# Attention scores with tokens on the partitions in a fused attention and expert kernel

## The chip, the cores and the metric

The kernel runs on 1 core of one Trainium2 chip. The metric is the device time of one execution in microseconds (us): the median of several runs of the kernel before is 1126.33 us (three runs, 1125.7 to 1126.88). One more execution was recorded by the hardware profiler, and every row shown below comes from that one.

## The reference, cut to what matters

Three layers follow one another. The change touches only the first, an attention over 32 memory slots. The inputs q, k and phi are the drawn ones times 64, 64 and 2.859.

```python
# q, k, v: (4, 8, 576, 64)   phi: (4, 8, 576, 32)   batch, head, token, dim / slot
a = softmax of phi over the 32 slots
k_m = einsum('bhsm,bhsd->bhmd', a, k)
v_m = einsum('bhsm,bhsd->bhmd', a, v)
scores = scale * matmul(q, k_m^T)                 # (4, 8, 576, 32)
scores = scores - max(scores, axis=-1)
attn = exp(scores)
attn = attn / (sum(attn, axis=-1) + 1e-9)
x = matmul(attn, v_m)                             # then to (2304, 512)
# layer 2, 2304 tokens, 512 -> 2048 -> 512
h = maximum(x @ w_in, 0);  x = (h * h) @ w_out
# layer 3, four experts, 512 -> 1024 -> 512, weighted by the normalised domain_probs
out += p[:, e] * (maximum(x @ w1[e], 0) @ w2[e])
```

## The kernel before

The 32 pairs of batch and head are worked in eight groups g of four heads (two groups to a batch b). In each group 4 heads times 32 slots make 128 rows. The softmax of the scores runs over the 32 slots, so it wants the slots along the free dimension and the tokens on the partitions, while what the next layer reads (atts, the attention weights, split into a rounded part and a rest) wants the slots on the partitions and the 576 tokens along the free dimension.

A group is a generator in two parts. The first (letter F in the order below) is lines 131 to 184: the softmax of phi, its five transposes on TensorE (143), the memories k_m and v_m (150), their transposes (167), and the scores (180). The scores come out with the 128 rows of heads and slots on the partitions and 288 tokens at a time along the free dimension, in one bank of tag score and one of tag fold. VectorE turns each bank at once by 32x32 blocks into st (184), and both banks are free again. The second part (letter B) is lines 186 to 203: the maximum over 32 slots (187), its subtraction (188), the exponential on ScalarE (191), the sum (193), the division (194 to 196), the block transposes back into at (200), the rounded copy on ScalarE (202) and the rest of it (203). Lines 188 and 203 stand on GpSimd from group 4 on, line 196 from group 3 on.

PSUM has banks by tag: three of moe, one of turn, one of memory, one of score, two of fold.

The string PROGRAM orders stage 0. Its other letters are: W, one chunk of the weights of layer 2, turned from 64-bit floats by seven VectorE instructions (lines 217 to 229, some with a split at 244 and 245); A, fold(0, b), which multiplies v_m of a batch into w_in (344 to 351, two banks of tag fold); U, first(0, j), which runs layer 2 on 288 tokens for a slab of 256 hidden units: lines 372 to 381 (hidden units, their square and its split), and lines 393 to 399 (the product with w_out), put off in the list pend. A batch's U reads its folded weights and the atts of both of its groups. Stage 1 and later run layer 2 on the other slabs, in which no attention is left, and then layer 3.

The loads run in one queue, SyncE's: phi (99), k and v (115), q (124), 64-bit weights (237). The string FIRST_LOADS names the first ten, and the function front(g) issues those of a group that are not yet there.

The program text gives the order in which work is offered. The order on each engine is the framework's plan: in the trace VectorE has instructions of W, of B and of U mixed. On each engine instructions then run strictly in the planned order.

The shares p of the experts are loaded behind stage 0 (770) and normalised by four small VectorE instructions (773 to 776). They are read in layer 3 alone.

Of the kernel before, what the change touches and what calls it, by code (L numbers as in the profile page):

```python
# [31 lines left out]
NB = 512  # L32
# [7 lines left out]
def tile_kernel(  # L40
# [24 lines left out]
    def bank(tag):  # L65
        return (ps if tag in ("moe", "score") else ps_one).tile([128, 512], F32, tag=tag, name=tag, bufs=BANKS[tag])
# [15 lines left out]
    yacc = acc.rearrange("p (k n) -> p k n", k=KT)  # L82


    FIRST_LOADS = "p0 p1 r0 k0 r1 q1 q0 k1 r2 r3"

    PROGRAM = (
        "F0 W W F1 W W B0 A0 B1 F2 F3 U0 U1 A1 B2 B3 F4 W B4 F5 B5 A2 U2 U3 W "  # L90
        "F6 F7 U4 W B6 W A3 B7 U5 U6 U7"
    )


# [2 lines left out]
    def load_phi(att, g):  # L97
        ph = att.tile([128, S], F32, tag="ph", name=f"ph{g}", bufs=2)
        nc.sync.dma_start(out=ph, in_=phiT[g])
        return ph  # L100
# [27 lines left out]
    def attention(att, g):  # L128
# [43 lines left out]
            nc.scalar.copy(bt[rows, :, e * M:(e + 1) * M], ktv[rows, 0, :, e, :])  # L172
        rows = slice(hg * D, (hg + 1) * D)
        nc.scalar.copy(vt[rows, b], kt[rows, 128:])
        st = att.tile([128, S // 32, 32], F32, tag="st", name="st", bufs=2)
        stf = st.rearrange("p j m -> p (j m)")
        for z in range(2):
            sc = bank("score" if z == 0 else "fold")
            for pr in range(2):
                nc.tensor.matmul(  # L180
                    sc[pr * 64:(pr + 1) * 64, :HS], bt[:, pr, :], qt[pr][:, z * HS:(z + 1) * HS],
                    start=True, stop=True,
                )
            nc.vector.transpose(out=stf[:, z * HS:(z + 1) * HS], in_=sc[:, :HS])
        yield
        mx = att.tile([128, S // 32], F32, tag="mx", name="mx")
        nc.vector.reduce_max(out=mx, in_=st, axis=AX.X)
        (nc.gpsimd if g >= 4 else nc.vector).tensor_tensor(
            out=st, in0=st, in1=mx.unsqueeze(2).to_broadcast([128, S // 32, 32]), op=ALU.subtract
        )  # L190
        nc.scalar.activation(st, st, AF.Exp, scale=1.0 / math.sqrt(D))
        sm = att.tile([128, S // 32], F32, tag="sm", name="sm")
        nc.vector.reduce_sum(out=sm, in_=st, axis=AX.X)
        nc.vector.tensor_scalar_add(sm, sm, 1e-9)
        nc.vector.reciprocal(sm, sm)
        (nc.gpsimd if g >= 3 else nc.vector).tensor_tensor(
            out=st, in0=st, in1=sm.unsqueeze(2).to_broadcast([128, S // 32, 32]), op=ALU.mult
        )
        at = att.tile([128, S], F32, tag="at", name="at", bufs=1)
        nc.vector.transpose(out=at, in_=stf)  # L200
        hi = atts[b][:, hg]
        nc.scalar.copy(hi, at)
        (nc.gpsimd if g >= 4 else nc.vector).tensor_tensor(out=atts[b][:, 2 + hg], in0=at, in1=hi.bitcast(F32), op=ALU.subtract)  # L203

    F_MIN = float(np.array(896 << 20, np.uint32).view(np.float32))
    F_MAX = float(np.array((1150 << 20) | 0xFFFFF, np.uint32).view(np.float32))
# [517 lines left out]
    with tc.tile_pool(name="bdp", bufs=1) as bdp, tc.tile_pool(name="cv", bufs=1) as cv, \  # L727
# [5 lines left out]
            nc.gpsimd.memset(t, 0.0)  # L733
        with tc.tile_pool(name="att", bufs=2) as att, tc.tile_pool(name="hp1", bufs=2) as hp, \
                tc.tile_pool(name="tmp1", bufs=1) as tmp:
            at = {}

            def front(g):
                if g not in phs:
                    phs[g] = load_phi(att, g)  # L740
                if g not in kvs:
                    kvs[g] = load_kv(att, g)
                if g not in qs:
                    qs[g] = load_q(g)
                at[g] = attention(att, g)
                next(at[g])

            for t in FIRST_LOADS.split():
                i = int(t[1])
                if t[0] == "p":  # L750
                    phs[i] = load_phi(att, i)
                elif t[0] == "k":
                    kvs[i] = load_kv(att, i)
                elif t[0] == "q":
                    qs[i] = load_q(i)
                else:
                    raws[i] = load64(i)
            for t in PROGRAM.split():
                i = int(t[1]) if len(t) > 1 else 0
                if t[0] == "F":  # L760
                    front(i)
                elif t[0] == "B":
                    next(at[i], None)
                elif t[0] == "W":
                    next(ws)
                elif t[0] == "A":
                    fold(0, i)
                else:
                    first(0, i, (hp, tmp), lambda: bank("moe"))
            nc.sync.dma_start(out=p_sb, in_=probs)  # L770
            flush()

        nc.vector.reduce_sum(out=p_sum, in_=p_sb, axis=AX.X)
        nc.vector.tensor_scalar_add(p_sum, p_sum, 1e-9)
        nc.vector.reciprocal(p_sum, p_sum)
        nc.vector.tensor_tensor(
            out=p_sb, in0=p_sb, in1=p_sum.unsqueeze(2).to_broadcast([128, NT // 128, E]), op=ALU.mult
        )
        with tc.tile_pool(name="hp2", bufs=2) as hp, tc.tile_pool(name="tmp2", bufs=2) as tmp:
            bk = lambda: bank(next(CYCLE1))  # L780
            for b in range(B):
# [9 lines left out]
        with tc.tile_pool(name="ring", bufs=1) as rp, tc.tile_pool(name="tmp3", bufs=2) as tmp:  # L791
            ring = [rp.tile([128, KT, RING], F32R, name=f"ring{i}") for i in range(2)]
            for s in range(2, N1):
                last = s + 1 == N1
                for j in range(2 * B):
                    first(s, j, (ring, tmp), bk)
                    if not last:
# [130 lines left out]
```

## Time and profile before

| | before |
|---|---|
| median of three runs | 1126.33 us (1125.7 to 1126.88) |
| the profiled execution | 1126.93 us, span 1125.2 us |
| TensorE busy | 1098.6 us (98%) |
| VectorE busy | 854.3 us (76%) |
| ScalarE busy | 586.8 us (52%) |
| GpSimd busy | 21.0 us (2%) |
[...]

The span is what lies between the first and the last instruction; 1.7 us of the profiled execution lie outside it. A busy share says how much of a stretch an engine had an instruction in work. For TensorE the ends of matmuls are modelled, so a busy TensorE need not be one at full rate; the weight loads (PEld) are listed beside it. The rows in the section below come from views of this one trace: busy time by stretch, instructions in order of time, and groups of equal instructions.

### The profile page before, as it was taken

The numbers are of one execution on the slowest core, as the hardware profiler recorded it, in microseconds if no ns is written. First come the engines' busy times: TensorE is split into PE (matmuls) and PEld (weight loads), VectorE is DVE, ScalarE is ACT, GpSimd is POOL, SyncE is SP. The second block draws the span as 40 slices with busy tenths as digits, with TensorE's granted clock in tenths as the row PEclk, the third lists the DMA queues.
The fourth block names the chain that finished last, engine by engine and source line by source line (L and its number), as shares of the span: only waits on it lengthen the run. The fifth ranks groups of instructions, "written<-read, shape, count | busy, mean of one in ns | idle before, by whom it ended". The sixth has DMA issues, their size and how long they took to land.

```text
span 1125.2 us, 16430 instructions
## 1 busy us (share of the span) xinstructions
PE 1098.6 (98%) x6150; PEld 936.3 (83%) x6150; DVE 854.3 (76%) x1478; ACT 586.8 (52%) x1164; POOL 21.0 (2%) x22
## 2 busy tenths in 40 slices
PE   5899999999999999999999999999999999999998
PEld 3567898998999988888888888888888888888887
DVE  6898989886345768888898786866766677776767
ACT  3777665665456465444444443455554554554551
POOL 0032000000000000000000000000000000000000
PEclk9799999999999999999999999999999999999999
DMA  9761212221020068776777766455544555554423
GB/s 328 226 206 57 76 58 75 78 92 39 1 95 1 38 269 306 281 286 257 267 290 281 268 238 233 157 198 188 191 162 154 183 174 178 178 198 170 150 94 112
DMA packets 59727, 192.22 MB, mean 171 GB/s; under 512 B 6648, under 2 KB 8696, under 8 KB 59648
## 3 DMA queue, kind: packets, MB, share of 16 engines
q1 hardware_dynamic: 59648, 191.18, 47.9%
q8 instruction: 48, 0.79, 0.3%
q14 instruction: 31, 0.25, 0.1%
HBM read 119.31 MB, written 71.84 MB: 170 GB/s over the span
## 4 chain that ended last, share of the span: by engine, by line
PE 87%; DVE 7%; ACT 3%; DMA 1%; issue 1%; POOL 1%; SPq 0%; ACTq 0%; POOLq 0%
PE moe L519 23%; PE two L636 13%; PE fold L485 8%; PE moe L393 7%; PE two L671 4%; PE score L519 4%; PE two L690 4%; PE turn L485 4%; PE memory L485 4%; PE moe L372 3%; PE turn L393 3%; PE memory L393 2%; PE score L393 2%; PE memory L372 1%; PE fold L344 1%; PE score L372 1%
## 5 line engine op out<-in xcount | busy, mean ns | idle before, releaser
L519 PE MATMUL moe<-mem,f 128*128 128x512 f32 x576 | 146.1, 389 | 0.0
L519 PEld LDWEIGHTS moe<-mem,f 128*128 128x128 f32 x576 | 107.9, 188 | 22.6 <-DVE mem L412 0.2
L643 DVE TENSOR_TENSOR acc<-two,acc 128x1024 f32<-128x1024 f32 x56 | 68.6, 1224 | 64.3 <-PE two L636 63.7
L519 PE MATMUL moe<-mem,ws 128*128 128x512 f32 x384 | 98.0, 390 | 0.0
L485 PE MATMUL fold<-w,g 128*128 128x512 f32 x384 | 97.6, 389 | 0.0
L636 PE MATMUL two<-gt,f 128*128 128x512 f32 x360 | 88.9, 389 | 0.0
L485 PEld LDWEIGHTS fold<-w,g 128*128 128x128 f32 x384 | 72.1, 188 | 15.0
L519 PEld LDWEIGHTS moe<-mem,ws 128*128 128x128 f32 x384 | 71.8, 188 | 15.3 <-DVE c L565 0.2
L393 PE MATMUL moe<-ring,wo 128*128 128x384 f32 x432 | 80.9, 335 | 0.0
L636 PEld LDWEIGHTS two<-gt,f 128*128 128x128 f32 x360 | 67.6, 188 | 14.2
L641 ACT COPY acc<-two 128x1024 f32<-128x1024 f32 x49 | 49.6, 1013 | 50.4 <-PE two L636 50.4
L393 PEld LDWEIGHTS moe<-ring,wo 128*128 128x128 f32 x432 | 75.1, 188 | 0.0
L372 PE MATMUL moe<-mem 128*128 128x288 f32 x432 | 72.8, 303 | 1.4 <-POOL mem L203 0.8
L372 PEld LDWEIGHTS moe<-mem 128*128 128x128 f32 x432 | 62.1, 191 | 12.4 <-issue 6.5
L381 DVE TENSOR_TENSOR ring<-g,ring 128x288 fp32r<-128x288 f32 x96 | 43.3, 455 | 31.6 <-ACT ring L380 31.6
L379 ACT ACTIVATE g<-r 128x288 f32<-128x288 f32 x128 | 57.1, 446 | 4.0 <-DVE gl L381 2.2
L530 ACT COPY cc<-moe 128x512 f32<-128x512 f32 x65 | 38.3, 589 | 25.5 <-PE moe L519 25.5
L498 DVE SCALAR_TENSOR_TENSOR acc<-fold,p_sb,acc 128x512 f32<-128x512 f32 x60 | 44.8, 747 | 8.5 <-PE fold L485 8.2
L671 PEld LDWEIGHTS two<-mem,f 128*128 128x128 f32 x384 | 48.2, 191 | 1.2
L485 PE MATMUL turn<-w,g 128*128 128x512 f32 x192 | 49.0, 390 | 0.0
L519 PE MATMUL moe<-mem,w 128*128 128x512 f32 x192 | 48.9, 389 | 0.0
L485 PE MATMUL memory<-w,g 128*128 128x512 f32 x192 | 48.7, 389 | 0.0
(190 smaller groups left out, 2278.6 us busy)
## 6 DMA issues: line engine op xcount, KB each, us to landing
f<-kept SPq DMA_DIRECT2D x128, 512.0 KB, 4.0
kept<-w SPq DMA_DIRECT2D x64, 512.0 KB, 2.9
kept<-ws SPq DMA_DIRECT2D x32, 512.0 KB, 3.8
kept<-mem SPq DMA_DIRECT2D x32, 512.0 KB, 3.3
raw<-in_wts SPq DMA_DIRECT2D x28, 512.0 KB, 3.2
ra<-in_wts SPq DMA_DIRECT2D x16, 512.0 KB, 4.9
rb<-in_wts SPq DMA_DIRECT2D x16, 512.0 KB, 3.9
kv<-in_kv SPq DMA_DIRECT2D x24, 256.0 KB, 4.1
```

Of the source, the lines that this page charges most:

```text
L372: nc.tensor.matmul(ph[:, :HS], folded[b][:, lw + hg, fc], atts[b][:, rx + hg, cs], start=(i == 0), stop=(i == 5))
L379: nc.scalar.activation(g, r, AF.Square)
L381: nc.vector.tensor_tensor(out=gl[:, f], in0=g, in1=gh[:, f].bitcast(F32), op=ALU.subtract)
L393: nc.tensor.matmul(po[:, :n], w[:, lw], rg[:, f], start=(i == 0), stop=(i == 3 * nf - 1))
L485: nc.tensor.matmul(po, g[f][:, lg, at:at + 128], w[:, rw], start=(i == 0), stop=(i == 3 * NF2 - 1))
L498: nc.vector.scalar_tensor_tensor(out=oa, in0=po, scalar=pe, in1=oa, op0=ALU.mult, op1=ALU.add)
L519: nc.tensor.matmul(po, wb[lw][k], xb[:, rx, k], start=(first and i == 0), stop=(i == 5), skip_group_check=not first,)
L636: nc.tensor.matmul(po[:, a], w[:, lw, o + a * 128:o + (a + 1) * 128], g[xb][:, rx], start=(i == 0 and not seeded), stop=(i == 2), skip_gro ...
L641: nc.scalar.copy(m, po)
L643: nc.vector.tensor_tensor(out=m, in0=po, in1=m, op=ALU.add)
L671: nc.tensor.matmul(two[:, f, :NR], w[f][:, lw, k * 128:(k + 1) * 128], x[:, rx, k], start=(i == 0), stop=(i == 3 * KT - 1),)
L690: nc.tensor.matmul(po[:, a], g[:, f, lg, a * 128:(a + 1) * 128], w[:, rw], start=(i == 0), stop=(i == 3 * NF2 - 1))
```

## The change

The scores are now computed with the tokens on the partitions: five blocks of up to 128 tokens, and for each block two matmuls in which q is the stationary operand and bt, the 64 columns of a pair of heads, the moving one. Four blocks lie in the bank of tag score, the fifth (64 tokens) in one of tag fold. Both banks are now held until the second part of the group has read them. There the maximum and its subtraction are taken from PSUM, once for four blocks and once for the fifth. The exponential, the sum and the division run over 640 instead of 576 elements of each partition, all of it on VectorE and ScalarE. Then five TensorE transposes bring the weights back into two banks of tag fold, from which ScalarE makes the rounded copies and VectorE the rests. No block transposes are left on VectorE, and GpSimd has none of this work.

Three things come with it. PROGRAM names the loads too, at places of their own, and its order is another: a W stands ahead of F0, U0 ahead of A1, the last W behind U7; q of groups 0 and 1 is loaded ahead of the second weight chunk. The loads of front(g) and FIRST_LOADS are gone. And the load and the normalisation of p stand at the start of the last slab of layer 2 instead of behind stage 0.

```diff
-    FIRST_LOADS = "p0 p1 r0 k0 r1 q1 q0 k1 r2 r3"
     PROGRAM = (
-        "F0 W W F1 W W B0 A0 B1 F2 F3 U0 U1 A1 B2 B3 F4 W B4 F5 B5 A2 U2 U3 W "
-        "F6 F7 U4 W B6 W A3 B7 U5 U6 U7"
+        "p0 p1 r0 k0 q0 q1 r1 k1 r2 r3 W F0 W W F1 W B0 A0 B1 q2 p2 k2 F2 p3 k3 B2 q3 F3 U0 A1 B3 p4 k4 q4 U1 F4 r4 W B4 p5 k5 r5 q5 F5 U2 U3 A2 B5 W p6 k6 q6 F6 p7 k7 q7 F7 U4 r6 W r7 B6 A3 B7 U5 U6 U7 W"
     )
...
-        st = att.tile([128, S // 32, 32], F32, tag="st", name="st", bufs=2)
-        stf = st.rearrange("p j m -> p (j m)")
-        for z in range(2):
-            sc = bank("score" if z == 0 else "fold")
+        NC = len(CH)
+        st = sts[g % 2]
+        sf = st.rearrange("p c m -> p (c m)")
+        sc = [bank("score"), bank("fold")]
+        for c, (s0, n) in enumerate(CH):
             for pr in range(2):
                 nc.tensor.matmul(
-                    sc[pr * 64:(pr + 1) * 64, :HS], bt[:, pr, :], qt[pr][:, z * HS:(z + 1) * HS],
-                    start=True, stop=True,
+                    sc[c // 4][:n, (c % 4) * 128 + pr * 64:(c % 4) * 128 + (pr + 1) * 64],
+                    qt[pr][:, s0:s0 + n], bt[:, pr, :], start=True, stop=True,
                 )
-            nc.vector.transpose(out=stf[:, z * HS:(z + 1) * HS], in_=sc[:, :HS])
         yield
-        mx = att.tile([128, S // 32], F32, tag="mx", name="mx")
-        nc.vector.reduce_max(out=mx, in_=st, axis=AX.X)
-        (nc.gpsimd if g >= 4 else nc.vector).tensor_tensor(
-            out=st, in0=st, in1=mx.unsqueeze(2).to_broadcast([128, S // 32, 32]), op=ALU.subtract
-        )
-        nc.scalar.activation(st, st, AF.Exp, scale=1.0 / math.sqrt(D))
+        mx = att.tile([128, NC, 4], F32, tag="mx", name="mx")
+        for z, (rows, cs) in enumerate(((slice(0, 128), slice(0, 4)), (slice(0, nlast), slice(4, NC)))):
+            n = (cs.stop - cs.start) * 4
+            x = sc[z][rows, :n * 32].rearrange("p (c m) -> p c m", m=32)
+            m = mx[rows, cs].rearrange("p c h -> p (c h)")
+            nc.vector.reduce_max(out=m, in_=x, axis=AX.X)
+            nc.vector.tensor_tensor(
+                out=st[rows, cs.start * 4:cs.stop * 4], in0=x, in1=m.unsqueeze(2).to_broadcast([rows.stop, n, 32]),
+                op=ALU.subtract,
+            )
+        nc.scalar.activation(sf, sf, AF.Exp, scale=1.0 / math.sqrt(D))
...
-        (nc.gpsimd if g >= 3 else nc.vector).tensor_tensor(
-            out=st, in0=st, in1=sm.unsqueeze(2).to_broadcast([128, S // 32, 32]), op=ALU.mult
+        (nc.gpsimd if g >= 8 else nc.vector).tensor_tensor(
+            out=st, in0=st, in1=sm.unsqueeze(2).to_broadcast([128, NC * 4, 32]), op=ALU.mult
         )
-        at = att.tile([128, S], F32, tag="at", name="at", bufs=1)
-        nc.vector.transpose(out=at, in_=stf)
-        hi = atts[b][:, hg]
-        nc.scalar.copy(hi, at)
-        (nc.gpsimd if g >= 4 else nc.vector).tensor_tensor(out=atts[b][:, 2 + hg], in0=at, in1=hi.bitcast(F32), op=ALU.subtract)
+        at = [bank("fold"), bank("fold")]
+        for c, (s0, n) in enumerate(CH):
+            nc.tensor.transpose(at[c // 4][:, (c % 4) * 128:(c % 4) * 128 + n], sf[:n, c * 128:(c + 1) * 128], ident[:n, :n])
+        for z, (c0, c1) in enumerate(((0, NB), (NB, S))):
+            nc.scalar.copy(atts[b][:, hg, c0:c1], at[z][:, :c1 - c0])
+            nc.vector.tensor_tensor(
+                out=atts[b][:, 2 + hg, c0:c1], in0=at[z][:, :c1 - c0], in1=atts[b][:, hg, c0:c1].bitcast(F32),
+                op=ALU.subtract,
+            )
...
-            nc.sync.dma_start(out=p_sb, in_=probs)
             flush()
-        nc.vector.reduce_sum(out=p_sum, in_=p_sb, axis=AX.X)
...
+                if last:
+                    nc.sync.dma_start(out=p_sb, in_=probs)
+                    nc.vector.reduce_sum(out=p_sum, in_=p_sb, axis=AX.X)
...
```

## Rows read from the trace of the kernel before

**Rows 1.** Busy time by stretch; columns named in the first line, (x) are instructions.
```profile
core 0: us, PE busy (x) PEld busy (x) DVE busy (x) ACT busy (x) POOL busy (x), PEclk, DMA share, GB/s
20.00:30.00 10.00, 5.57 (x35) 2.70 (x35) 9.31 (x19) 4.59 (x11) 0.00 (x0) 0.78 0.99 351
30.00:40.00 10.00, 7.68 (x60) 4.55 (x60) 9.01 (x21) 6.07 (x16) 0.00 (x0) 0.50 0.57 175
44.00:100.00 56.00, 50.72 (x494) 36.97 (x493) 50.44 (x103) 41.47 (x113) 17.59 (x13) 1.00 0.55 176
100.00:110.00 10.00, 10.00 (x77) 9.96 (x77) 8.01 (x18) 8.63 (x23) 0.00 (x0) 1.00 0.32 104
...
270.00:280.00 10.00, 10.00 (x71) 9.97 (x65) 3.90 (x8) 4.25 (x11) 0.00 (x0) 1.00 0.01 2
```

**Rows 2.** TensorE in order of time: start, us, line, operation, [idle before <-releaser].
```profile
31.53 1.12 PE L143 MATMUL turn<-ident,ph 128*128 128x128 f32 x4 [4.41 <-ACT ph L134]
...
68.83 0.27 PE L143 MATMUL memory<-ident,ph 128*64 128x128 f32 x1
68.94 0.60 PE L143 MATMUL turn<-ident,ph 128*128 128x128 f32 x4
...
83.95 0.71 PE L180 MATMUL score<-acc,bdk 128*64 128x288 f32 x4
...
99.73 0.80 PE L372 MATMUL moe<-mem 128*128 128x288 f32 x4 [0.80 <-POOL mem L203]
```

**Rows 3.** VectorE and one GpSimd instruction in order of time, 60 to 106 us.
```profile
60.87 1.26 DVE L219 TENSOR_SCALAR ca<-cm 128x512 uint32<-128x512 uint32 x1
69.58 1.68 DVE L381 TENSOR_TENSOR gl<-g,gh 128x288 fp32r<-128x288 f32 x1
72.15 1.65 DVE L226 SCALAR_TENSOR_TENSOR cm<-raw,cm 128x512 f32<-128x512 uint32 x1
75.66 1.09 DVE L774 TENSOR_SCALAR p_sum<-p_sum 128x18 f32<-128x18 f32 x1
89.05 0.93 DVE L222 SCALAR_TENSOR_TENSOR ca<-raw,ca 128x512 uint32<-128x512 uint32 x1
90.80 1.42 POOL L203 TENSOR_TENSOR mem<-at,mem 128x576 fp32r<-128x576 f32 x1 [1.36 <-ACT mem L202]
90.91 1.85 DVE L226 SCALAR_TENSOR_TENSOR cm<-raw,cm 128x512 f32<-128x512 uint32 x1
98.62 1.59 DVE L222 SCALAR_TENSOR_TENSOR ca<-raw,ca 128x512 uint32<-128x512 uint32 x1
100.92 0.69 DVE L226 SCALAR_TENSOR_TENSOR cm<-raw,cm 128x512 f32<-128x512 uint32 x1
101.61 0.46 DVE L381 TENSOR_TENSOR gl<-g,gh 128x288 fp32r<-128x288 f32 x1
104.64 0.43 DVE L219 TENSOR_SCALAR ca<-cm 128x512 uint32<-128x512 uint32 x1
105.10 0.69 DVE L222 SCALAR_TENSOR_TENSOR ca<-raw,ca 128x512 uint32<-128x512 uint32 x1
```

**Rows 4.** Groups by line, 0 to 300 us: count | busy us, mean ns | idle before.
```profile
L351 DVE TENSOR_TENSOR mem<-fold,mem 128x512 fp32r<-128x512 f32 x22 | 14.1, 683 | 1.9 <-ACT mem L350 1.9
L200 DVE STREAM_TRANSPOSE at<-st 128x576 f32<-128x576 f32 x8 | 6.2, 774 | 1.5 <-POOL st L196 1.4
L193 DVE TENSOR_REDUCE sm<-st 128x18 f32<-128x576 f32 x8 | 6.0, 749 | 1.9 <-ACT st L191 1.5
L187 DVE TENSOR_REDUCE mx<-st 128x18 f32<-128x576 f32 x8 | 5.9, 740 | 0.0
L184 DVE STREAM_TRANSPOSE st<-score 128x288 f32<-128x288 f32 x8 | 3.8, 475 | 3.5 <-PE score L180 2.5 <-PE fold L180 1.0
L188 DVE TENSOR_TENSOR st<-st,mx 128x576 f32<-128x576 f32 x4 | 3.0, 755 | 0.0
L203 DVE TENSOR_TENSOR mem<-at,mem 128x576 fp32r<-128x576 f32 x4 | 3.0, 754 | 0.1
```

**Rows 5.** ScalarE's smallest copy out of PSUM, as a group, 0 to 300 us.
```profile
L146 ACT COPY en<-memory 64x128 f32<-64x128 f32 x8 | 2.1, 260 | 0.5 <-PE memory L143 0.5
```

## Predicting the time of the changed kernel

> **What bounds the kernel now.** I read the busy shares of the whole span first: TensorE 98%, so most of the kernel is TensorE's own work, and only time in which it lacks work can be won. Next come the stretches [rows 1], to find that time. From 100 us on TensorE shows 10.00 of 10 and its weight loads 9.96 of 10: that is an engine without gaps. Between 44 and 100 us it shows 50.72 of 56, and its weight loads only 36.97 of 56. So 5.3 us are plainly idle there, and perhaps as much as 56 x (1 - 36.97/56) = 19 us are not at full rate. From 20 to 40 us it is worse: 5.57 and 7.68 busy of 10 each, at a granted clock of 0.78 and 0.50. In the same stretches VectorE is busy 9.31 and 9.01 of 10, and 50.44 of 56: as long as attention lasts, VectorE is nearly full and TensorE waits, and all that the change touches lies in this stage 0. Two rows name the waiting [rows 2]: 4.41 us ahead of the transposes at 31.53 (they wait for an exponential that VectorE's maximum of phi releases), and 0.80 us at 99.73 for GpSimd's line 203 of the last group. From there to the end the work is fixed. The change therefore comes down to two questions: does TensorE reach its gapless state earlier or later than 99.7 us, and how much more of its own work has it then done?
>
> The third view is VectorE in order of time [rows 3]. Six instructions there take far longer than the same instruction a few us later: 1.26 against 0.43, 1.68 and 1.65 against 0.46 and 0.69, 0.93 against 0.69, 1.85 against 0.69, 1.59 against 0.69. Together the excess is 0.83 + 1.22 + 0.96 + 0.24 + 1.16 + 0.90 = 5.3 us. The row of line 203 on GpSimd (90.80 to 92.22) shows why: VectorE's line 226 begins at 90.91 and ends at 92.76, its own 0.69 behind GpSimd's end less a little. VectorE stood still while GpSimd worked. So VectorE's 50.44 us between 44 and 100 hold 5.3 us that are no work.
>
> **The change part by part.**
>
> *GpSimd's instructions go.* Thirteen of them, 17.59 us [rows 1], leave the stage. With them goes VectorE's standstill, 5.3 us, and VectorE's waits for them: 1.4 us ahead of line 200, and about half of the 1.5 us ahead of line 193 (half, because there it waits for the exponential, which waited for GpSimd's line 188) [rows 4]. Sum about -7.4 us of VectorE's time.
>
> *VectorE's own work.* Of groups 0 to 2 it did two block transposes of 0.475 (line 184), 0.740 (187), 0.755 (188), 0.749 (193), 0.755 (196, of the form of 188), 0.774 (200) and 0.754 (203): 5.48 us a group. Of group 3 4.72, as line 196 was GpSimd's; of groups 4 to 7 3.21 (0.95 + 0.740 + 0.749 + 0.774) [rows 4]. Altogether 16.4 + 4.7 + 12.8 = 34.0 us. The new instructions are priced by size: 0.46 us for 288 elements [rows 3] and 0.755 for 576 [rows 4] give 0.165 us and 1.02 ns per element. So 512 elements cost 0.69, 128 cost 0.30, 640 cost 0.82 and 64 cost 0.23. A group is then 2 x (0.69 + 0.30) for maximum and subtraction, 0.82 each for sum and division, and 0.69 + 0.23 for the rests: 4.54 us, 36.3 us for eight. That is +2.3 us: -0.9 us in each of the first three groups, +1.3 us in each of the last four.
>
> Does a source in PSUM cost more? Line 351 reads PSUM and takes 0.683 for 512 elements [rows 4]; my line gives 0.69 for operands in SBUF. I take no surcharge. [...]
>
> *The shares p.* Line 774 alone takes 1.09 us in stage 0 [rows 3], and three small ones stand beside it. They go to the last slab, where VectorE is busy 3.90 of 10 and the DMA engines 0.01 [rows 1], so the load finds SyncE's queue and VectorE free. Gain in stage 0 1.1 us, cost later none; if that cover were gone it would be the same 1.1 us and a wait for one load.
>
> VectorE's sum is -7.4 + 2.3 - 1.1 = -6.2 us, about a third of it ahead of 44 us.
>
> *TensorE's work.* Transposes: four in 0.60, one alone in 0.27 [rows 2], so the next of a row costs 0.11 us. Five a group are 0.55 us. Scores: before, a group has 8 matmuls of 288 columns, four in 0.71 (83.95) [rows 2], so 1.1 us with two such rows and the second row's start overlapped. Now it has 10 products, each of two instructions as before, so 20 loads of up to 128 columns with 64 columns streamed. No row shows such a pair. Its upper neighbour is the transpose, also 128 columns loaded but 128 streamed, 0.11 us; below, if the load hid wholly, half of that, 0.055. So 1.1 to 2.2 us; I take 2.2, as the load is what both have in common. A group adds 0.55 + 1.1 = 1.6 us (0.55 at least), eight groups 13 us (4.4 at least). At a granted clock of 0.50 the price is about double: the row at 31.53 shows 1.12 us where the one at 68.94 shows 0.60 [rows 2].
>
> [...]
>
> How much of it is hidden? Between 44 and 100 us lie about five groups' scores and six groups' transposes: 5 x 1.1 + 6 x 0.55 = 8.8 us. They meet 5.3 us of shown idle time and up to 19 us of time below full rate [rows 1]. The middle, 12 us, covers them, though not by much. Ahead of 44 us there is idle time enough (4.41 us at one place), and the cost there is latency, covered by the W chunks with which VectorE is full anyway.
>
> *ScalarE* makes two copies instead of one and 64 elements more in the exponential: at most 0.26 us, the smallest copy out of PSUM [rows 5], a group, 2 us in all. It is busy 41.47 of 56 [rows 1]; with that cover gone the 2 us would stand on the path.
>
> *New waits.* The bank of tag score is now held from F until B's subtraction; before, line 184 freed it. F(g+1)'s score matmuls wait for two VectorE instructions of B(g), at F1 ahead of B0 and F7 ahead of B6, 1.4 us each at most; TensorE's U work and VectorE's W work can stand in. The transposes wait in TensorE's planned order for VectorE's division, with everything queued behind them on TensorE, the put-off products of U above all. Where the plan puts them too early, TensorE stops; the nearest such waits are of 0.80 us [rows 2]. I put half of that on six groups, +2 us. A fold A(b) now shares two fold banks with scores and transposes; I take nothing for it, 0 to 2 us.
>
> *Order of loads.* The same ten first loads run, q two places earlier, the second weight chunk two later. The DMA engines are full up to 30 us (0.99 [rows 1]), so what one gains another loses: 0, with -2 to +2 us.
>
> *Sum.* VectorE's -6.2 us is what stage 0 can shrink by; +2 us for TensorE waiting at the transposes; its added work hidden. -4.2 us against the profiled execution's 1126.93 gives 1122.7 us. The median lies 0.6 us below that execution, so 1122.1; I say 1122.5.
>
> **The rivals.**
>
> *TensorE becomes the bound (slower).* Place: 44 to 100 us. If only the 5.3 us of shown idle time can be used, 8.8 - 5.3 = +3.5 us, whatever VectorE saves. If the transposes of six groups also stop it for 0.80 us each, +8.3 us. It decides once the usable slack is below 8.8 us. For it: VectorE's freed time helps only work that TensorE then has to do. Against it: weight loads at 36.97 of 56. It gives 1130 to 1135, 1131 as the middle. [...]
>
> *Both cancel.* VectorE's gain is given back in TensorE's waits, the sum is within 2 us: 1124.3 to 1128.5. It is also what comes if the plan keeps the old pace because the held score bank ties F(g+1) to B(g).
>
> [...]
>
> **How the numbers follow.** The forecast 0.41, the clock too 0.12, cancelling 0.20, TensorE the bound 0.27. About 0.2% (2.25 us) is what a measurement of this kernel can tell from no change. The first two are faster: 0.53. Same: 0.20. Slower: 0.27. The range leaves out the outer half of the last rival and the best of the clock: 1115 to 1132. The forecast's own range is 1119 to 1124.
>
> **What would show it.** Right: no VectorE instruction above its usual time in stage 0; VectorE's groups at 4.5 us; TensorE without gaps before 96 us, weight loads above 0.75 between 44 us and there; five transposes at 0.6 us and score pairs at or below 0.11 us. Wrong: TensorE idle at the new transposes or at score matmuls waiting for a bank; score pairs at 0.13 us and more; a gapless state that begins later than 100 us with VectorE below 85%; instructions of VectorE that read PSUM clearly above 0.69 us for 512 elements. The forecast also fails if stage 0's pace is set by the loads, which I priced at nothing.

## The result, and the profile after

The changed kernel takes 1133.15 us (median of four runs, 1128.32 to 1135.49), the kernel before 1126.01 us on the same chip: a ratio of 1.0057, 95% interval 1.0037 to 1.0077. The first experiment repeats it with five runs: 1133.14 against 1125.5 us, 1.0069 [1.0057, 1.0082]. So the change made the kernel slower by some 7 us, where 4 us of gain were forecast.

The executions of the changed kernel differ among themselves by up to 7 us. The one that was profiled first ("after", 1128.32 us, span 1126.5) is the shortest of all nine; the one profiled in the repeat ("the repeat", 1134.51 us, span 1132.7) is the longest of its five, 1.4 us above their median. Both are shown.

First the busy time of each engine over the whole span, the first section of the page; after, then the repeat:

```profile
PE 1107.2 (98%) x6286; PEld 952.2 (85%) x6286; DVE 848.2 (75%) x1491; ACT 588.0 (52%) x1172; POOL 3.8 (0%) x11
```

```profile
PE 1111.7 (98%) x6286; PEld 956.3 (84%) x6286; DVE 848.1 (75%) x1491; ACT 588.2 (52%) x1172; POOL 3.8 (0%) x11
```

Take TensorE's busy time from the span, and what is left is its idle time. Before it is 1125.2 - 1098.6 = 26.6 us. In the repeat it is 1132.7 - 1111.7 = 21.0 us. So idle time fell by 5.6 us and busy time rose by 13.1 us, and the sum is the 7.5 us by which the spans differ. For after the same account is -7.3 and +8.6. The two run the same instructions, so busy time is not work alone: it also holds what the low level of TensorE's clock costs (below, the same sixteen products take 3.65 us in the repeat and 2.23 in after). VectorE is busy 6.1 us less, and the end comes no earlier for it.

Then the stretches, in the columns of [rows 1]; after:

```profile
20.00:30.00 10.00, 7.59 (x47) 5.23 (x48) 9.46 (x21) 4.45 (x9) 0.00 (x0) 0.57 0.71 266
30.00:40.00 10.00, 8.75 (x91) 7.34 (x90) 7.70 (x20) 5.82 (x19) 0.00 (x0) 0.92 0.64 195
44.00:100.00 56.00, 55.45 (x550) 46.30 (x549) 45.64 (x111) 40.68 (x115) 0.00 (x0) 1.00 0.52 164
```

and the repeat:

```profile
20.00:30.00 10.00, 7.89 (x62) 5.97 (x51) 7.71 (x17) 3.05 (x7) 0.00 (x0) 1.00 0.93 330
44.00:100.00 56.00, 55.02 (x572) 46.29 (x572) 43.82 (x108) 40.69 (x115) 0.00 (x0) 1.00 0.60 186
```

Between 44 and 100 us TensorE is now busy 55 of 56 us instead of 50.72, and VectorE 44 to 46 instead of 50.44. The bound of this stretch has moved from VectorE to TensorE. The weight loads fill only 46.3 of the 56, though the engine has no gap to speak of.

TensorE in order of time shows where the early microseconds go (columns as in [rows 2]). Line 176 are the scores, 201 the transposes back, 345 the fold, 373 layer 2's first product. The kernel before (180, 344, 372 there):

```profile
15.11 1.24 PE L180 MATMUL score<-acc,bdk 128*64 128x288 f32 x4
16.12 1.18 PE L180 MATMUL fold<-acc,bdk 128*64 128x288 f32 x4
...
21.98 1.02 PE L180 MATMUL score<-acc,bdk 128*64 128x288 f32 x4 [0.61 <-issue]
22.73 1.24 PE L180 MATMUL fold<-acc,bdk 128*64 128x288 f32 x4
23.89 1.82 PE L344 MATMUL fold<-wf,vt 64*32 64x256 f32 x16
25.64 1.47 PE L372 MATMUL moe<-mem 128*128 128x288 f32 x9
...
38.37 1.23 PE L180 MATMUL score<-acc,bdk 128*64 128x288 f32 x4
...
84.48 0.65 PE L180 MATMUL fold<-acc,bdk 128*64 128x288 f32 x4
```

the repeat:

```profile
14.38 3.68 PE L176 MATMUL score<-bdk,acc 128*128 128x64 f32 x16 [0.60 <-ACT bdk L167]
17.99 0.69 PE L176 MATMUL fold<-bdk,acc 128*64 128x64 f32 x4
...
23.80 3.65 PE L176 MATMUL score<-bdk,acc 128*128 128x64 f32 x16 [0.56 <-issue]
27.38 0.69 PE L176 MATMUL fold<-bdk,acc 128*64 128x64 f32 x4
28.00 1.12 PE L201 MATMUL fold<-ident,st 128*128 128x128 f32 x4
30.51 0.37 PE L201 MATMUL fold<-ident,st 64*128 64x64 f32 x1 [1.40 <-DVE mem L204]
31.77 1.97 PE L345 MATMUL fold<-wf,vt 64*32 64x256 f32 x16 [0.89 <-DVE mem L204]
33.87 2.53 PE L373 MATMUL moe<-mem 128*128 128x288 f32 x9
...
43.01 2.00 PE L176 MATMUL score<-bdk,acc 128*128 128x64 f32 x16
```

and after, with two rows of a late group:

```profile
12.55 2.00 PE L176 MATMUL score<-bdk,acc 128*128 128x64 f32 x16 [0.69 <-ACT bdk L167]
...
19.89 2.23 PE L176 MATMUL score<-bdk,acc 128*128 128x64 f32 x16 [0.56 <-issue]
...
26.44 1.97 PE L345 MATMUL fold<-wf,vt 64*32 64x256 f32 x16 [0.89 <-DVE mem L204]
28.53 2.53 PE L373 MATMUL moe<-mem 128*128 128x288 f32 x9
...
37.00 2.00 PE L176 MATMUL score<-bdk,acc 128*128 128x64 f32 x16
...
84.47 2.00 PE L176 MATMUL score<-bdk,acc 128*128 128x64 f32 x16
86.40 0.45 PE L176 MATMUL fold<-bdk,acc 128*64 128x64 f32 x4
91.26 0.80 PE L201 MATMUL fold<-ident,st 128*128 128x128 f32 x5
```

The same sixteen pairs of load and product take 2.00 us in one place and 3.65 in another: that is TensorE's clock at its two levels (after has 2.00 us at 37.00, where the clock is listed as 1.00 by a record; a trace below has 3.65 us at a listed clock of 0.50). The column of the granted clock does not show it for the repeat, since that trace has no clock record before 39.5 us, and a stretch without one is listed as 1.00. By the records the high level holds almost to the end, from 31.7 us on in after, from 39.5 in the repeat and from 42.7 before. Of the repeat's group 0 all twenty take 18.68 - 14.38 = 4.30 us; of the late group at 84.47 they take 2.38. The old form took 17.30 - 15.11 = 2.19 us at the low level (1.24 and 1.18 us for its two rows of four; the same four take 1.24 at 22.73, where the clock is listed as 0.50, and 0.65 at 84.48).

From group 0's first score to layer 2's first product is one chain. It goes through group 0's scores, group 1's scores, group 0's transposes, and the fold:

| | before | after | repeat |
|---|---|---|---|
| group 0's scores to group 1's | 6.87 | 7.34 | 9.42 |
| group 1's scores to the fold | 1.91 | 6.55 | 7.97 |
| fold to the first product | 1.75 | 2.09 | 2.10 |
| sum | 10.53 | 15.98 | 19.49 |

Of the repeat's 9 us more, 4.4 are the scores of the two groups (2.11 and 2.3 us each), and 3.7 are group 0's transposes and what waits behind them. These run from 28.07 to 31.77, after group 1's scores on TensorE, where before the fold followed the scores at once. Two waits, 1.40 and 0.89 us, lie inside them, both until VectorE's line 204 has read a bank of tag fold; group 1's scores hold the other one.

From group 2's scores to the end of the span the kernel before has 1125.2 - 38.37 = 1086.8 us, after 1126.5 - 37.00 = 1089.5, the repeat 1132.7 - 43.01 = 1089.7. So there are two parts. The late one costs 2.7 to 2.9 us in both executions; such a remainder is good to some 2 us, as the last experiment, with the old form and the old order, has 1124.8 - 39.84 = 1085.0. The early one costs 4.6 us in the repeat and gains 1.4 in after. Of the 6.0 us between these two, 3.2 are the scores of groups 0 and 1 at the low level (1.78 and 1.42), and 1.8 are a later start of group 0's scores (14.38 against 12.55). The later start comes from a load. ScalarE's line 218 reads the first weights and stands ahead of the copy (139) that TensorE waits for. First after, then the repeat:

```profile
5.84 0.65 ACT L218 ACTIVATE cm<-acc 128x512 f32<-128x512 f32 x1
```

```profile
7.64 0.66 ACT L218 ACTIVATE cm<-acc 128x512 f32<-128x512 f32 x1 [1.81 <-DMA acc<-in_wts]
```

VectorE in groups, after, 0 to 300 us (columns as in [rows 4]):

```profile
L223 DVE SCALAR_TENSOR_TENSOR ca<-raw,ca 128x512 uint32<-128x512 uint32 x28 | 19.3, 688 | 0.5
...
L382 DVE TENSOR_TENSOR gl<-g,gh 128x288 fp32r<-128x288 f32 x32 | 14.5, 452 | 4.2 <-ACT gh L381 3.2 <-ACT g L380 0.9
...
L196 DVE TENSOR_TENSOR st<-st,sm 128x640 f32<-128x640 f32 x8 | 6.5, 811 | 0.0
...
L204 DVE TENSOR_TENSOR mem<-fold,mem 128x512 fp32r<-128x512 f32 x8 | 5.5, 689 | 1.3 <-ACT mem L203 1.1
L186 DVE TENSOR_REDUCE mx<-score 128x16 f32<-128x512 f32 x8 | 5.5, 689 | 7.7 <-PE score L176 7.7
L187 DVE TENSOR_TENSOR st<-score,mx 128x512 f32<-128x512 f32 x8 | 5.4, 672 | 0.0
...
L187 DVE TENSOR_TENSOR st<-fold,mx 64x128 f32<-64x128 f32 x8 | 2.2, 274 | 0.0
```

The stretched instructions of [rows 3] are gone: lines 223 and 382 stand at 688 and 452 ns in the mean. VectorE's new wait is on TensorE: 7.7 us ahead of the maximum, where 2.5 stood ahead of line 184 before [rows 4].

### The profile page after: what moved, and what is told of

It reads as the page before. It is cut to its first block, busy times and chain, and to the rows that moved or that the text cites. A ratio compares the mean times of both kernels' runs of the same rounds, so it can differ in the third digit from the quotient of the medians.

```text
span 1126.5 us, 16718 instructions
## 1 busy us (share of the span) xinstructions
PE 1107.2 (98%) x6286; PEld 952.2 (85%) x6286; DVE 848.2 (75%) x1491; ACT 588.0 (52%) x1172; POOL 3.8 (0%) x11
## 4 chain that ended last, share of the span: by engine, by line
PE 93%; DVE 3%; ACT 2%; DMA 2%; issue 0%; ACTq 0%; SPq 0%; DVEq 0%
PE moe L520 23%; PE two L637 13%; PE moe L394 9%; PE fold L486 8%; PE moe L373 5%; PE two L672 4%; PE two L691 4%; PE turn L486 4%; PE memory L486 4%; PE score L520 4%; PE turn L394 2%; PE score L394 2%; PE memory L394 2%; PE fold L345 1%; PE memory L373 1%; PE score L373 1%
```

## The experiments

Each label is one kernel. In all of them the ratio is to the kernel before, run on the same chip. Its median was 1125.5 us beside e1 to e4, 1126.81 beside e5 to e8, and 1126.12 beside e9 to e12. Differences in us are taken to these, and two kernels are compared by their differences.

**The change again, and its two halves.** The first kernel is the change unaltered.

> The changed kernel once more, nothing altered, for its spread and a second trace. Theory A (TensorE's own added work, 8 groups x 1.9 us = 15 us of weight loads and transposes, uses up the slack of stage 0): the same time in each execution, near 1128, as the added work does not vary. Theory B (how long TensorE stays at the lower clock in the first 40 us differs from execution to execution, and this kernel is more exposed): times spread over some 7 us as in the first comparison, and a trace of a long execution shows score or fold matmuls at the slow rate for longer than up to 31 us, with the later stages unchanged.

Measured: 1133.14 us (1132.3 to 1134.51), 1.0069 [1.0057, 1.0082]. Its trace is the repeat, above.

The next takes the new order of the program, the new places of the loads and the late p, with the old attention:

```diff
-    FIRST_LOADS = "p0 p1 r0 k0 r1 q1 q0 k1 r2 r3"
-    PROGRAM = (the old order)
+    PROGRAM = (the new order, loads named in it)
     # attention(): as before
```

> The new order, loads by name and the late shares p, with the old attention (block transposes, GpSimd from groups 3 and 4 on). Theory A: no more TensorE work, so within 3 us of the kernel before, 1124 to 1129. Rival C (the new order and its loads cost the time, not the form): 1130 or more, and TensorE idle between 44 and 100 us well above 5.3 us.

Measured: 1131.71 us, 1.0058 [1.0044, 1.0071]. The order alone loses 6.2 us with the old form: the time is rival C's, though TensorE's idle time between 44 and 100 us is 6.3 us and not well above 5.3. Its TensorE, in order of time, waits at places where the kernel before does not:

```profile
76.65 0.79 PE L367 MATMUL moe<-mem 128*128 128x288 f32 x4 [1.77 <-ACT mem L345]
...
99.71 0.66 PE L367 MATMUL moe<-mem 128*128 128x288 f32 x3 [1.28 <-ACT acc L394]
```

Idle time of TensorE over its span is 1132.5 - 1102.6 = 29.9 us, 3.3 more than before, and its busy time is 4.0 us more for the same instructions. Much of the 4.0 is the clock, behind the second of these waits (columns of [rows 1]):

```profile
100.00:110.00 10.00, 9.46 (x46) 8.47 (x46) 7.63 (x14) 5.87 (x15) 1.46 (x1) 0.66 0.15 54
```

TensorE gets through 46 instructions here at a mean granted clock of 0.66, where before it got through 77 at 1.00 [rows 1]. The low level lasts 6.8 us, from 101.4 to 108.2, and half of that, 3.4 us, is an estimate of what it cost in this execution. From group 2's scores (39.29) to the end this execution has 1093.2 us, 6.4 more than before, so the loss lies there. What else this order does to the old form was not taken apart.

And the converse, the new attention in the old order with the old loads and the old p:

```diff
     # attention(): as after
-    PROGRAM = (the new order, loads named in it)
+    FIRST_LOADS = "p0 p1 r0 k0 r1 q1 q0 k1 r2 r3"
+    PROGRAM = (the old order)
```

> The new attention (scores with tokens on partitions, five transposes back, no GpSimd) in the old order, with the old loads and shares p behind stage 0. Theory A: slower than before by 2 to 8 us, 1128 to 1134, TensorE nearly without gaps from 60 us on and VectorE waiting for score matmuls. Rival C: equal to the kernel before or faster, as VectorE has 6 us less to do.

Measured: 1135.24 us (1132.77 to 1136.78), 1.0085 [1.0073, 1.0098], above all that was expected. So the form alone costs 9.7 us, and the new order takes 2 us of that back. The two do not add: 9.7 and 6.2 make 7.6 together.

**GpSimd out, nothing else.**

```diff
-        (nc.gpsimd if g >= 4 else nc.vector).tensor_tensor(   # line 188; 196 and 203 likewise
+        nc.vector.tensor_tensor(
```

> The kernel before with lines 188, 196 and 203 on VectorE in all groups, nothing else altered. It tells what taking GpSimd out is worth by itself. My prediction's step (GpSimd holds VectorE up for 5.3 us, and VectorE waits 2.1 us for it) says: 13 instructions of 0.755 us more on VectorE, 9.8 us, less 7.4 us: about 2 us more VectorE time, but shorter chains per group; 1124 to 1128. If VectorE's time between 44 and 100 us is the bound, 1128.

Measured: 1129.63 us, 1.0037 [1.0024, 1.0049], 4.1 us slower. By the prediction's own terms VectorE takes 13 x 0.755 = 9.8 us over and gets 7.4 us back, a loss of 2.4 us. The sign is that, the size somewhat above. So GpSimd did more for the kernel before than it did harm, although VectorE stood still meanwhile (5.3 us by [rows 3]).

**The pairs' price, in all groups.** One product of 128 columns replaces the two of 64 for each block, so that ten loads a group fall away; the scores of the other two heads are left out.

```diff
-            for pr in range(2):
-                nc.tensor.matmul(
-                    sc[c // 4][:n, (c % 4) * 128 + pr * 64:(c % 4) * 128 + (pr + 1) * 64],
-                    qt[pr][:, s0:s0 + n], bt[:, pr, :], start=True, stop=True,
-                )
+            nc.tensor.matmul(
+                sc[c // 4][:n, (c % 4) * 128:(c % 4 + 1) * 128],
+                qt[0][:, s0:s0 + n], bt.rearrange("p a m -> p (a m)"), start=True, stop=True,
+            )
```

> The changed kernel with one score product per block of tokens instead of two: q of the first pair of heads stands for both pairs (so the scores of the other two heads are left out), 64 columns streamed become 128, 10 weight loads a group instead of 20. Theory A (TensorE's added work is the cost, early on the chain and later because TensorE is the bound): 10 pairs less, 0.12 us each at full clock and 0.225 at the low one seen in the longer execution: 2 x 2.2 us early plus 6 x 1.2 us later, up to 11 us less, 1122 to 1126. Rival D (the waits for banks and the plan's order cost it, not the pairs): less than 3 us, 1130 or more.

Measured: 1125.49 us (twelve runs, 1123.86 to 1126.96), 0.9991 [0.9981, 1.0001]: level with before. By the medians it is 1.3 us under before, where the change is 7.6 above, so 9.0 us less. The first section of its page:

```profile
PE 1102.6 (98%) x6206; PEld 945.7 (84%) x6206; DVE 846.7 (75%) x1491; ACT 588.0 (52%) x1172; POOL 3.8 (0%) x11
```

Idle time is 1123.7 - 1102.6 = 21.1 us, the same as the repeat's 21.0. Busy time is 9.1 us less than the repeat's, that is 0.114 us for each of the 80 loads and products saved. All of it comes off the end: TensorE has no room left.

This also says where VectorE's gain is. Against the order alone (busy 1102.6, idle 29.9) this kernel has the same busy time and 8.8 us less idle. The new form does relieve TensorE's waiting; the second half of the pairs then costs as much again.

**The pairs' price by place, from the old order.** The new form in groups 2 to 7 only, and in groups 0 and 1 only, order and loads as before (both forms use the changed kernel's fixed tiles for st):

```diff
+        if g >= 2:        # the second kernel: if g < 2
+            ...           # scores to rests as after
+            return
         ...               # as before
```

> Old order, the new form only in groups 2 to 7, groups 0 and 1 in the old form. The new form in all groups of this order took 1135.2. Theory E (the early chain of groups 0 and 1, on a TensorE at its low clock, costs 4 to 5 us of it): 1130 to 1131. If the later groups carry it all: 1135.

> Old order, the new form only in groups 0 and 1, the other six in the old form with GpSimd as before. Theory E: 4 to 5 us above the kernel before, 1130. If the later groups carry it all: 1125 to 1126, or below, as VectorE has 0.9 us a group less there.

Measured: 1132.94 us, 1.0064 [1.0049, 1.0078], for groups 2 to 7, and 1130.61 us, 1.0035 [1.0023, 1.0047], for groups 0 and 1. These are +6.1 and +3.8 us, 9.9 together, and the whole form in that order costs 9.7. So the loss has two places, and they add. Theory E's 1130 holds for the second kernel; the first lies between the two times expected, so the later groups carry more than it said. In the trace of the second kernel group 1's scores stand at the low level, and here the granted clock of the stretch says so too (columns of [rows 1]; then TensorE in order of time):

```profile
20.00:30.00 10.00, 7.13 (x39) 5.38 (x35) 6.11 (x13) 2.96 (x8) 0.00 (x0) 0.50 0.93 330
```

```profile
22.67 3.65 PE L182 MATMUL score<-bdk,acc 128*128 128x64 f32 x16 [0.56 <-issue]
```

**The pairs' price by place, from the new order.** The change with one product for two, in groups 0 and 1 only and in groups 2 to 7 only; the scores of two heads are left out in these groups.

```diff
             for pr in range(2):
+                ...   # one product for both, as above, where g < 2 (the second kernel: g >= 2)
```

> The changed kernel with one score product per block in groups 0 and 1 alone (q of the first pair stands for both there, so the scores of two of their four heads are left out). In the trace with one product in all groups, 8 pairs at the low clock took 2.08 us where 16 took 3.68, and the first U matmul came about 3 us earlier. Theory E (early chain at the low clock): 3 us off 1133, 1130. If the early pairs are covered by VectorE's work, as my prediction had it: 1133.

> The counterpart: one product in groups 2 to 7 alone (there two of four heads are left out). Theory A's late part (TensorE is the bound from 44 us on): 16 to 20 pairs at 0.12 us become 8 to 10 at about 0.14, some 0.9 us a group, 5 us off 1133, 1128; TensorE's busy share between 44 and 100 us falls below 0.98. If only the early chain counts: 1133.

Measured: 1130.53 us, 1.0036 [1.0022, 1.0050], and 1128.07 us (eleven runs), 1.0018 [1.0008, 1.0029]. These kernels are 4.4 and 2.0 us above the one before, where the change is 7.6 above. That is -3.2 and -5.7 us, 8.9 together, where all groups gave 9.0. In the first kernel group 0's eight products of the first bank stand at the low level at 2.08 us, as against 3.68:

```profile
15.06 2.08 PE L176 MATMUL score<-bdk,acc 128*128 128x128 f32 x8 [0.60 <-ACT bdk L167]
```

The late part can be worked out by price. In the half form a late group's scores take 1.52 us from start to end instead of 2.38; the rows are from the trace with all groups halved:

```profile
84.15 1.16 PE L175 MATMUL score<-bdk,acc 128*128 128x128 f32 x8
85.24 0.43 PE L175 MATMUL fold<-bdk,acc 128*64 128x128 f32 x2
```

Six groups save 6 x 0.86 = 5.2 us of TensorE's time. The medians give 5.7 us. The trace of this kernel has 1125.2 - 40.56 = 1084.6 us from group 2's scores to the end, 5.1 less than the repeat. Within these errors a microsecond of TensorE is a microsecond of the kernel there.

**Filler ahead of the scores.** To try whether more work on TensorE holds the clock up at groups 0 and 1, transposes of the identity into a bank of tag moe: 24 at the start and 16 in each of the two groups.

```diff
+    def spin(n):
+        d = bank("moe")
+        for _ in range(n):
+            nc.tensor.transpose(d[:, :128], ident, ident)
+    spin(24)
...
+        if g < 2:
+            spin(6)    # and 4 ahead of kvd, 6 ahead of bt
```

> The changed kernel with idle-filling transposes of the identity on TensorE: 24 at the start, while the first loads run, and 16 each in groups 0 and 1 where TensorE waits for ScalarE. They write a bank that nothing reads. Theory B (the low clock of the first 40 us costs 4 to 6 us in most executions, and the first profiled one had caught the high clock by chance): score pairs of group 0 at 0.12 us and times around 1128, all executions close together. Against B: the same 1133, or more by what the added transposes hold up.

Measured: 1144.82 us, 1.0161 [1.0142, 1.0181], 18.0 us above before and so 10 worse than the change. TensorE in order of time:

```profile
17.05 3.60 PE L189 MATMUL score<-bdk,acc 128*128 128x64 f32 x16
...
26.87 1.97 PE L189 MATMUL score<-bdk,acc 128*128 128x64 f32 x16 [0.23 <-issue]
...
31.77 1.09 PE L214 MATMUL fold<-ident,st 128*128 128x128 f32 x4 [2.56 <-DVE st L209]
```

Group 0's scores are still at the low level, with 3.60 us, and begin 2.7 us later than in the repeat; group 1's are at the high one, 1.97 instead of 3.65 us, and begin 3.1 us later. For the rest the high level stands at other places: the records have it from 6.5 to 13.3 us, ahead of group 0's scores, and again from 23.5 to 30.4 (0.82 in the mean of 20 to 30 us, 0.52 in that of 30 to 40). Then the low level holds until 57.7 us, where the repeat is at the high one from 39.5 on. The stretch from 44 to 100 us shows it (columns of [rows 1]):

```profile
44.00:100.00 56.00, 55.03 (x552) 45.23 (x545) 40.89 (x101) 36.27 (x101) 0.00 (x0) 0.88 0.59 190
```

The filler costs more than it gives, and so it does not tell what a higher clock at groups 0 and 1 alone would give. That stays open.

**Another bank for the fifth transpose.**

```diff
-        at = [bank("fold"), bank("fold")]
+        at = [bank("fold"), bank("moe")]
```

> The changed kernel with the fifth transpose's 64 tokens in a bank of tag moe instead of the second fold bank, nothing else altered. In the trace the fifth transpose of group 0 waits 1.40 us, and fold A0 0.89 us behind it, for VectorE to leave the fold bank, as group 1's scores hold the other. Rival D (the held banks cost part of it): 1 to 2.5 us off, 1131 to 1132. Theory A alone: no change, 1133; slower if U lacks the bank.

Measured: 1155.28 us, 1.0252 [1.0238, 1.0267], some 22 us worse than the change. The stretch, in the columns of [rows 1], and one row of TensorE:

```profile
44.00:100.00 56.00, 51.14 (x443) 42.18 (x441) 38.07 (x92) 32.13 (x88) 0.00 (x0) 0.78 0.51 168
```

```profile
52.85 3.68 PE L176 MATMUL score<-bdk,acc 128*128 128x64 f32 x16 [0.73 <-ACT bdk L167]
```

TensorE runs 443 instructions there instead of 572, at a mean granted clock of 0.78. Layer 2 takes its banks from tag moe as well; that the fifth transposes now compete with it is the likely cause, but it was not shown. What holding the score and fold banks costs stays open too.

**The late p alone.**

```diff
-            nc.sync.dma_start(out=p_sb, in_=probs)          # and its four VectorE instructions
+                if last:
+                    nc.sync.dma_start(out=p_sb, in_=probs)  # and the four, at the last slab
```

> The kernel before with the load and normalisation of p at the start of the last slab, nothing else altered. My prediction put this part at 1.1 us of VectorE's time gained in stage 0 and none lost later: 1125 against 1126. If the gain is not on the path: no difference that can be measured.

Measured: 1126.07 us (eleven runs), 0.9993 [0.9983, 1.0002]. No difference can be told, but the work was not moved either. VectorE runs the second of the four at 74.53 us here and at 73.89 in after (second row), where the kernel before runs it at 75.66 [rows 3]:

```profile
74.53 1.08 DVE L791 TENSOR_SCALAR p_sum<-p_sum 128x18 f32<-128x18 f32 x1
```

```profile
73.89 0.17 DVE L787 TENSOR_SCALAR p_sum<-p_sum 128x18 f32<-128x18 f32 x1
```

The edit changes the program text, and the framework's plan runs the work in stage 0 all the same; the load is issued at 63.2 us instead of 64.2. So no kernel here had a late p in time, and what one would gain stays untried. The rows show something else: the instruction itself takes 0.17 us. Here and before it takes 1.08 and 1.09 beside a GpSimd instruction (line 203, from 75.27 to 76.72 before), and with GpSimd out alone 0.18. So 0.9 us of it are the same standstill as in the other stretched rows.

No kernel that does the whole computation was measurably faster than the one before.

## Why the prediction was wrong

The forecast was 1122.5 us and the result is 1133.15, above the range of 1115 to 1132. The direction was wrong, and the rival that named it, TensorE as the bound at 1130 to 1135, gave the size. Its place, 44 to 100 us, holds only a part of the loss.

- **GpSimd's standstill: right as a reading, but it was no gain by itself.** No VectorE instruction is stretched any more (lines 223 and 382 at 688 and 452 ns in the mean). But with GpSimd out alone the kernel lost 4.1 us, as its work has to go somewhere.
- **VectorE's own work: right.** The groups give 0.689 + 0.271 for the maximum, 0.672 + 0.274 for the subtraction, 0.813 (line 193) and 0.811 for sum and division, 0.689 + 0.215 for the rests. That is 4.43 us against 4.54 predicted. That the prediction took no surcharge for a source in PSUM held: 689 and 672 ns for 512 elements out of PSUM, 688 for line 223, which reads SBUF.
- **TensorE's added work: a little low, and no busy time confirms it.** 13 us were predicted for eight groups. The repeat is busy 13.1 us more, but after, with the same instructions, 8.6, so the agreement is luck. By place, a late group's scores take 2.38 us where they took 1.18 before (83.95 [rows 2] to 85.13), and the transposes back 0.80: 2.0 us a group, 16 for eight, at the high level. A pair costs 0.12 us there (1.93 from 84.47 to 86.40, for 16) and not 0.11, and the five transposes 0.80 us and not 0.55 (0.27 for one alone [rows 2], so 0.13 for each further one). At the low level a pair costs 3.65 / 16 = 0.23 us; the prediction gave that doubling for transposes, and used it nowhere for the scores.
- **"The middle, 12 us, covers them": the first step that failed.** It took the mean of 5.3 us of shown idle time and 19 us that the weight loads' share of 36.97 in 56 seemed to leave. Only the shown idle time was there. Over the whole span the idle time fell by 5.6 us, and the busy time rose by 13.1. After the change TensorE is busy 55 of 56 us while its loads show 46.3, so here a load share of 83% went with an engine that had no gap, and the missing 17% were no free time. With the 5.3 us in its place, the prediction's own sum for this stretch is 8.8 - 5.3 = +3.5 us, and from group 2's scores on the two traces show +2.7 and +2.9. That these are so close is partly luck, as the order changed too: in the old order the new form in groups 2 to 7 cost 6.1 us. In groups 2 to 7 the pairs count one for one (5.2 us saved; 5.1 in the traces, 5.7 by the medians).
- **"Ahead of 44 us the cost is latency, covered by the W chunks": the second.** Groups 0 and 1 lie on the chain to the first product of layer 2, and TensorE has no work of layer 2 to put between (busy 7.89 of 10 from 20 to 30 us in the repeat). There latency is time: in the repeat the first product begins 8.2 us later (33.87 against 25.64), and 4.6 us of that are left at group 2's scores. VectorE's W chunks do not help TensorE's chain. Groups 0 and 1 alone account for +3.8 us in the old order, and in the new one half of their pairs alone for 3.2.
- **TensorE waiting at the transposes, +2 us: right that there is a price, wrong about its place.** In the later groups the transposes run without a wait (91.26: five in 0.80, none listed). The wait is in group 0, where the five stand behind group 1's scores, and the waits for banks are 1.40 and 0.89 us.
- **The clock, to which the prediction gave a chance of 0.12 for a gain: what it is worth by itself no run shows.** The granted clock of 30 to 40 us rose from 0.50 [rows 1] to 0.92 in after, and after is 6 us shorter than the repeat, of which 3.2 are the scores of groups 0 and 1. But in the repeat (3.65 us for sixteen), and in four more traces with the new form in groups 0 and 1 (twice 3.65; 2.04 and 2.02 for the eight of half the pairs, against 1.16 at the high level), the scores of group 1 run at the low level, and the new form has more work there. In two others they take 2.28 and 2.47 us, nearer to the 2.00 of the high one.
- **The late p (-1.1 us) and the order of loads (0):** the p term failed as a step, since its work stayed in stage 0, and 0.9 us of its 1.1 were GpSimd's standstill. For the order of the work, as against that of the loads, the prediction had no term. It is not nothing: with the old form the two together cost 6.2 us, with the new one they gain 2. Loads and order were not tried apart.

Most signs that were named as proof of the forecast came true: no stretched instruction on VectorE, its groups at 4.4 us, TensorE all but gapless long before 96 us, load share above 0.75. The two on price did not (transposes at 0.80, pairs at 0.12 us), and one sign of being wrong did, TensorE's wait for a bank in group 0. The signs that held showed that TensorE had become the bound, and not that the kernel had become shorter. A test for the sum would have been idle time given up against busy time added.

## What to carry to other kernels

Here work added to an engine that is busy 98% of the span was paid for beyond the idle time that the trace showed on it, and a load share below the busy share (46.3 of 56 us beside 55) was no slack. Where a form trades few long products for many short ones, count the weight loads, and price them at both clock levels (0.12 and 0.23 us a pair here) for the groups that come first, since here the chain to the first useful product had no cover. Freeing the engine that is second is worth what the first one then waits less: here 5.6 us of idle time, against 13.1 of busy time added. And a line moved in the program text need not move in time: look it up in the trace, as the late p shows.

## What the hardware showed that was not expected

- Twenty loads of up to 128 columns, with 64 columns streamed behind each, take 2.38 us at the high level and 4.30 us at the low one. The columns loaded weigh more in this than the columns streamed. At the low level a pair with 128 loaded and 64 streamed takes 0.22 us (23.80 to 27.38 in the repeat, for sixteen), one with 64 loaded and 64 streamed 0.155 (27.38 to 28.00, for four), and one with 128 loaded and 128 streamed 0.25 (15.06 to 17.06 in the half form of groups 0 and 1, for eight).
- The granted clock is listed as 1.00 in the repeat between 20 and 30 us, while sixteen pairs take 3.65 us there; with the same 3.65 another trace lists 0.50. The repeat's trace has no clock record before 39.5 us. The durations of equal instructions tell the level where the column has no record.
- Whether groups 0 and 1 find the high level changes from one execution to the next (their sixteen products take 2.00 and 2.23 us in after, 3.68 and 3.65 in the repeat): after and the repeat are the same kernel, and their spans differ by 6.2 us, in which the level and the 1.8 us of waiting for the first weights go together. Ahead of group 1's first transpose of phi, shortly before these scores, TensorE had waited 0.46 us in after and 2.31 in the repeat. What decides the level was not shown; in the trace with the filler, the one attempt to force it, group 1's scores alone have it (1.97 us, group 0's 3.60).
